# Maxima split on ACT and DVE, turned among the scores; the sums' input in five loads; a new order

## The chip, the cores and the metric

The kernel runs on one core of a Trainium2 chip. A core has a matrix engine (PE), three engines for element-wise work (DVE, ACT, POOL), a queue for transfers (SP) and 16 DMA engines. Times are microseconds of the device for one execution, and for a kernel the median of its runs.

## The reference

Attention over 8 batches of 8 heads with 576 positions of 64 columns, then a soft mixture of 8 experts with 4 slots each on the 4608 tokens of 512 columns:

```python
scores = scale * np.matmul(q, k.transpose(0, 1, 3, 2))
cum = np.cumsum(np.maximum(s, 0.0), axis=-1)
bias = -(cum[:, :, :, None] - cum[:, :, None, :])
scores = np.where(causal, -1000000000.0, scores + np.minimum(bias, 0.0))
scores = scores - np.max(scores, axis=-1, keepdims=True)
attn = np.exp(scores); attn = attn / (np.sum(attn, axis=-1, keepdims=True) + 1e-09)
x = np.matmul(attn, v)                       # heads side by side: 4608 x 512
logits = x @ phi                             # 4608 x 32
d = softmax over tokens of logits;  slot_input = d.T @ x
slot_out[e] = np.maximum(slot_input[e] @ w1[e], 0.0) @ w2[e]
out = (softmax over slots of logits) @ slot_out
```

The decay needs the running sums of s for every head before the first score can be formed, and the softmax needs each row's maximum before the scores that are exponentiated.

## The kernel before, in words

Two heads make a pair (32 pairs), and each pair's work is a set of steps. Head a of a pair lies in rows 64a to 64a + 63 of a tile, so a product over the 64 columns of a head uses half of the PE's rows, and two of them run side by side (tile shape 64*128 in the profile). q and k are cast to a rounded format on ACT (`cast`, L344), and what the rounding lost is kept by DVE (`low`, L349), one step each for q and k.

Each pair's scores are formed twice. First, in rounded numbers and with queries as rows, for the row maxima only (`mx`, L378, in four groups of which each fills two banks of PSUM); DVE takes the maxima (`red`, L389). The maxima, 5 chunks of 128 queries for two heads, are split into a rounded and a remaining part by two small operations on POOL (`f0`, L404 and L405), turned by the PE (`f1`; L425, one product on a tile of 128 rows and 64 columns; L421 for pair 0), copied by ACT (`f2`, L429) and moved by DMA into rows 32, 33, 96 and 97 of the tile `g`, whose rows 0, 1, 64 and 65 hold the running sums. Then the scores are formed again with keys as rows (`s`, L461, four products per block, the last with `g`), now less the maximum, and ACT exponentiates them (`ex`, L472). POOL clears what lies above the diagonal (`cut`, L479) and adds the blocks for the row sums (`z`, L507 to L513). The PE multiplies with v (`ax`, `a`: L560, L571, tile 128*64) and sums (`sm`, L599, 128*32), DVE scales the result (`nr`, L632), the PE turns it (`nat`) and forms logits (`lt`).

At the start s comes in by three loads (L202 to L204): heads 2 to 63 in rows 2 to 63, and heads 0 and 1 twice each into rows 0, 1 and 64, 65, which is where pair 0 wants them. DVE takes the maximum with zero (L227), the running sums (L228), their rounded part (L231) and writes `g` of pair 0 (L257); a POOL memset (L271) sets rows 32 and 33 of it to -1, after DVE's. The products of pair 0's maxima wait for both.

Six banks of PSUM go round in a ring for all products but the two longest-lived. The PE's order is given by a table of numbers (`PR`: first, phase, last); on the other engines a planner (`schedule`) runs through the steps with a duration each and takes the step that can start first, or the one with the smallest due time (also from `PR`). The outcome is written out as a fixed program per engine. Where the plan has the PE idle ahead of pair 0's weighted sums, filler products (L991) are put in.

## Time and profile before

| | us |
|---|---|
| median of 3 runs | 443.04 (441.56 to 446.37) |
| profiled execution | 437.39 |
| its span, first to last instruction | 435.4 |
| PE, DVE, POOL, ACT busy in the span | 413.4, 319.2, 281.7, 249.0 |
| first product that contains the sums | 12.5 |
| weights of the experts: first product | 373.5 |

A busy PE is a PE with products in flight; the ends of pipelined products are modelled, so the distance between two starts tells more of one product than its time. Idle time of an engine counts only where another one waits for it.

### The profile page before, as it was taken

Reading aid. Unit: us, or ns where it says so; the run is one execution under the profiler, and the core shown is the slowest. Engines: PE = TensorE matmul, PEld = TensorE weight load, DVE = VectorE, ACT = ScalarE, POOL = GpSimd, SP = SyncE. Lnnn points to the kernel's source line nnn. Section 1 sums busy time; section 2 is a strip of 40 time slices with the busy share of each in tenths; the row PEclk is TensorE's granted clock in tenths of the full one; section 3 lists DMA queues with packets and bytes.
Section 4 is the critical chain, followed back from the end, with each engine's and each line's share of the span. In section 5 each row is a group of like instructions: output and inputs, shape, how many; then the busy total and the mean of one; then the engine's idle time right before and its main releaser. Section 6 shows DMA issues by size and latency. Waiting matters only on the chain.

```text
span 435.4 us, 14712 instructions
## 1 busy us (share of the span) xinstructions
PE 413.4 (95%) x5708; PEld 302.1 (69%) x5708; DVE 319.2 (73%) x1039; ACT 249.0 (57%) x741; POOL 281.7 (65%) x389
## 2 busy tenths in 40 slices
PE   7899999999999999999999999999997999999990
PEld 7677777777687778777877687678775786345450
DVE  4899788878797889788978898789859555120570
ACT  2265766686667656765686577656773564111470
POOL 5769798968978788778877887679677930000000
PEclk9899999999999999999999999999999999999996
DMA  6317446762675257525853684253336879997898
GB/s 172 96 57 232 138 140 195 212 230 86 171 224 167 85 162 238 161 85 160 229 173 95 159 231 114 83 159 98 105 91 170 250 231 400 408 409 312 271 336 265
DMA packets 54174, 82.72 MB, mean 190 GB/s; under 512 B 5358, under 2 KB 41562, under 8 KB 54104
## 3 DMA queue, kind: packets, MB, share of 16 engines
q1 hardware_dynamic: 54104, 81.78, 60.0%
q8 instruction: 45, 0.74, 0.7%
q14 instruction: 25, 0.20, 0.2%
HBM read 71.39 MB, written 10.03 MB: 187 GB/s over the span
## 4 chain that ended last, share of the span: by engine, by line
PE 70%; DVE 10%; DMA 10%; issue 3%; POOL 2%; SPq 2%; ACT 1%; DVEq 0%; ACTq 0%
PE s L461 19%; PE y L571 15%; PE mx L378 10%; DMA arena<-rs 5%; PE m L1060 3%; PE sum L599 3%; PE po L1094 3%; PE m L1031 3%; DVE w L349 3%; DVE junk L389 3%; PE nat L640 3%; DMA rs<-sr 2%; PE sl L844 2%; DMA arena<-in_s_dram 2%; PE lt L713 1%
## 5 line engine op out<-in xcount | busy, mean ns | idle before, releaser
L472 ACT ACTIVATE arena<-s 128x288 f32<-128x288 f32 (+4 forms) x384 | 119.6, 393 | 74.4 <-PE s L461 73.2
L389 DVE CUSTOM_DVE_ANT_0 junk<-mx,mask 128x448 uint8<-128x448 f32 (+2 forms) x320 | 118.6, 424 | 17.7 <-PE mx L378 16.8
L461 PE MATMUL s<-w 64*128 64x288 f32 (+4 forms) x1152 | 110.6, 299 | 3.1 <-DVE mx L389 2.9
L571 PE MATMUL y<-arena 128*64 128x512 f32 (+4 forms) x640 | 97.2, 430 | 0.0
L461 PEld LDWEIGHTS s<-w 64*128 64x128 f32 (+1 forms) x1152 | 87.5, 176 | 12.2 <-DVE mx L389 5.8
L479 POOL TENSOR_SCALAR_AFFINE_SELECT arena<-arena 128x256 f32<-128x256 f32 (+1 forms) x160 | 67.0, 437 | 32.5 <-ACT arena L472 32.3
L349 DVE TENSOR_TENSOR w<-arena,w 128x576 fp32r<-128x576 f32 x64 | 83.9, 1330 | 3.5 <-ACT w L344 3.3
L507 POOL TENSOR_TENSOR arena<-arena 128x896 f32<-128x896 f32 x31 | 67.1, 2163 | 10.2 <-PE sum L599 8.5
L378 PE MATMUL mx<-w 64*128 64x288 f32 (+4 forms) x384 | 64.1, 317 | 2.0 <-ACT w L344 1.4
L461 PE MATMUL s<-g 64*128 64x288 f32 (+4 forms) x384 | 64.0, 291 | 0.2 <-DMA g<-hl 0.2
L571 PEld LDWEIGHTS y<-arena 128*64 128x64 f32 x640 | 39.4, 136 | 33.9 <-issue 26.0
L509 POOL TENSOR_TENSOR arena<-arena 128x640 f32<-128x640 f32 x31 | 55.3, 1784 | 2.0
L378 PE MATMUL mx<-g,ones 64*128 64x288 f32 (+4 forms) x384 | 55.2, 303 | 1.0 <-POOL g L271 1.0
L344 ACT CAST w<-arena 128x576 fp32r<-128x576 f32 x64 | 41.4, 676 | 16.9 <-DMA arena<-in_qk_dram 16.9
L378 PEld LDWEIGHTS mx<-w 64*128 64x128 f32 x384 | 39.8, 185 | 13.6 <-issue 4.3
L461 PEld LDWEIGHTS s<-g 64*128 64x128 f32 (+1 forms) x384 | 42.7, 177 | 1.2 <-DMA g<-hl 0.5
L632 DVE TENSOR_TENSOR arena<-arena 128x576 f32<-128x576 f32 x30 | 32.5, 1082 | 13.7 <-DMA arena<-rs 13.5
L378 PEld LDWEIGHTS mx<-g,ones 64*128 64x128 f32 x384 | 39.9, 187 | 1.7 <-POOL g L271 1.3
L511 POOL TENSOR_TENSOR arena<-arena 128x384 f32<-128x384 f32 x31 | 34.6, 1115 | 0.5
L389 DVE CUSTOM_DVE_ANT_0 junk<-mx,mask,mx 128x288 uint8<-128x288 f32 x64 | 30.0, 504 | 2.0 <-PE mx L378 1.8
L389 DVE DVE_READ_ACCUMULATOR2_ANT mx<- 128x1 f32 x384 | 31.0, 81 | 0.0
L404 POOL TENSOR_SCALAR mh<-mx 128x10 fp32r<-128x10 f32 x32 | 17.2, 539 | 16.0 <-DVE mx L389 15.7
(168 smaller groups left out, 539.2 us busy)
## 6 DMA issues: line engine op xcount, KB each, us to landing
arena<-in_qk_dram SPq DMA_DIRECT2D x32, 576.0 KB
pre<-in_w_dram SPq DMA_DIRECT2D x35, 512.0 KB
arena<-in_w_dram SPq DMA_DIRECT2D x18, 512.0 KB
arena<-rs SPq DMA_DIRECT2D x60, 144.0 KB
arena<-in_v_dram SPq DMA_DIRECT2D x32, 256.0 KB
out_dram<-arena SPq DMA_DIRECT2D x11, 512.0 KB
ww<-in_w_dram SPq DMA_DIRECT2D x7, 512.0 KB
wg<-in_w_dram SPq DMA_DIRECT2D x4, 512.0 KB
```

The source lines that it names most:

```text
L344: nc.scalar.copy(part(i), st["raw", p][:, i, :])
L349: nc.vector.tensor_tensor(part(2 + i), st["raw", p][:, i, :], part(i).bitcast(F32), op=ALU.subtract)
L378: nc.tensor.matmul(ps[a][:, d:d + hi - lo], l[r], t[r, KO + lo:KO + hi], start=t is w, stop=t is gt)
L389: nc.vector.tensor_tensor_reduce(out=junk[:, a, k:k + w], in0=ps[:, d:d + w], in1=mask[:, o:o + w], scale=1.0, scalar=m[:, a, 4:5] if i == ...
L461: nc.tensor.matmul(ps[a][0:n, d:d + hi - lo], t[r, ko + 128 * j:ko + 128 * j + n], t[r, qo + lo:qo + hi], start=x == 0, stop=x == 3)
L472: nc.scalar.activation(st["p", p][0:n, a, o + lo:o + hi], ps[0:n, d:d + hi - lo], AF.Exp, bias=0.0, scale=0.125)
L479: nc.gpsimd.affine_select(d, d, pattern=[[0, 2], [1, n]], compare_op=ALU.is_ge, fill=0.0, base=0, channel_multiplier=-1)
L507: eng.tensor_tensor(z[:, :, 128:576], pt[:, :, 128:576], pt[:, :, 576:1024], op=ALU.add)
L509: eng.tensor_tensor(z[:, :, 256:576], z[:, :, 256:576], pt[:, :, 1024:1344], op=ALU.add)
L511: eng.tensor_tensor(z[:, :, 384:576], z[:, :, 384:576], pt[:, :, 1344:1536], op=ALU.add)
L571: nc.tensor.matmul(y[r, lo - 64:512], vt[:, j, r], st["p", p][:, g, OFF[j] + lo - 128 * j:OFF[j] + 576 - 128 * j], start=(j == 0), stop=(j ...
L632: nc.vector.tensor_tensor(u, u, st.pop(("r", p)), op=ALU.mult)
```

## The change

Five things change. (1) s comes in by five loads: heads 0 and 1 twice each, then 30, 30 and 2 heads; heads 32 and 33 move to rows 66 and 67, rows 32 and 33 hold -1 throughout, and so DVE writes the whole of `g` of pair 0 and the POOL memset behind it is gone. The first maxima wait for DVE's set-up alone. The sums' copy to memory goes in three transfers. (2) The maxima are split by ACT (`fh`, a copy) and DVE (`f0`, a subtraction). (3) They are turned by two products on half rows, one for each half of 64 queries, into two banks; ACT copies them in two pieces. (4) The planner keeps one time for a port that DVE steps with two inputs in SBUF and POOL steps hold in turn: a step marked `port` starts no earlier than the last such one ended. Durations of steps are changed in a dozen places (by up to 0.8 us). (5) All numbers of the table `PR` are new, so the order is new on every engine.

```diff
-PR = dict(load=-2708.8403, load_v=1055.8902, cast=(823.0986, 1016.176), cum=-2520.1417,
...
+PR = dict(load=1107.499, load_v=998.6149, cast=(1514.9315, 1120.6562), cum=574.2308,
...
 PER = 1000
...
     mode = None
-    dma = 0
+    dma = port = 0
     index = {k: i for i, k in enumerate(ops)}
...
                 gap = 0 if e != "PE" else max(2, o["ldw"] - tail) if o["mode"] == mode else 100 + o["ldw"]
-                r = max(ready[k], f + gap)
+                r = max(ready[k], f + gap, port if o["port"] else 0)
                 n = o["bank"]
...
         free[e] = end
+        if o["port"]:
+            port = end
         if e == "PE":
...
-    begin = reg("p", NPB - 1)[0:66]
+    begin = reg("p", NPB - 1)[0:68]
     s_sb, ones_s, cum = begin[:, 0:S], begin[:, S:2 * S], begin[:, 1600:1600 + S]
-    nc.sync.dma_start(out=s_sb[2:64], in_=s[2:64])
-    nc.sync.dma_start(out=s_sb[0:2], in_=s[0:1].broadcast_to([2, S]))
-    nc.sync.dma_start(out=s_sb[64:66], in_=s[1:2].broadcast_to([2, S]))
+    for a in range(2):
+        nc.sync.dma_start(out=s_sb[64 * a:64 * a + 2], in_=s[a:a + 1].broadcast_to([2, S]))
+    heads = [(2, 2, 30), (34, 34, 30), (66, 32, 2)]
+    for r, h, n in heads:
+        nc.sync.dma_start(out=s_sb[r:r + n], in_=s[h:h + n])
+    nc.vector.memset(s_sb[32:34], 0.0)
     nc.vector.memset(ones_s, 1.0)
...
         mx.append(one.tile([128, 2, NCH], F32, name=f"mx{i}"))
-    mhs = [one.tile([128, 64], F32R, name=f"mh{i}") for i in range(2)]
-    ident1 = one.tile([128, 128], F32R, name="ident1")
-    nc.vector.tensor_copy(ident1, ident)
+    mhs = [one.tile([128, 128], F32R, name=f"mh{i}") for i in range(2)]
+    half1 = one.tile([128, 64], F32R, name="half1")
+    for a in (0, 64):
+        nc.vector.tensor_copy(half1[a:a + 64], ident[a:a + 64, a:a + 64])
     odd = one.tile([128, 1], F32, name="odd")
     nc.vector.scalar_tensor_tensor(odd, ident[:, 1:2], -1.0, ident[:, 65:66], op0=ALU.mult, op1=ALU.subtract)
     nc.vector.tensor_scalar(s_sb, s_sb, 0.0, 8.0, op0=ALU.max, op1=ALU.mult)
+    nc.vector.memset(s_sb[32:34, 0:1], -1.0)
     nc.vector.tensor_tensor_scan(out=cum, data0=ones_s, data1=s_sb, initial=0.0,
...
     ginit(0)
-    nc.vector.scalar_tensor_tensor(gs[0][0:66, KO:], cumhl[:, 0, :], odd[0:66], cum, op0=ALU.mult, op1=ALU.add)
+    nc.vector.scalar_tensor_tensor(gs[0][0:66, KO:], cumhl[0:66, 0, :], odd[0:66], cum[0:66], op0=ALU.mult, op1=ALU.add)
     ws = []
...
         nc.gpsimd.memset(reg("p", i).rearrange("p (a x) -> p a x", a=2)[64:128, :, 1536:1600], 0.0)
-    nc.gpsimd.memset(gs[0][32:34, KO:].bitcast(F32), -1.0)
     OFF = [0, 576, 1024, 1344, 1536]
     st = {}
     ops = {}
     live = {}
-    def op(key, eng, ns, prio, fn, after=(), bank=0, frees=None, dma=0, ldw=107, tail=107, mode=0, lat=0):
+    def op(key, eng, ns, prio, fn, after=(), bank=0, frees=None, dma=0, ldw=107, tail=107, mode=0, lat=0, port=0):
...
         ops[key] = dict(eng=eng, ns=ns, prio=round(t, 6), fn=fn, after=[a for a in after if a is not None], bank=bank,
-                        frees=frees or [], dma=dma, pt=prio, ldw=ldw, tail=tail, mode=mode, lat=lat)
+                        frees=frees or [], dma=dma, pt=prio, ldw=ldw, tail=tail, mode=mode, lat=lat,
+                        port=port or eng == "POOL" and key[0] not in ("set", "gi"))
...
             op(("cast", p, i), "ACT", 565, (tu, ("cast", i)), (cast, i), [("load", p)] + war)
-            op(("low", p, i), "DVE", 820, (t0, ("low", i)), (low, i), [("cast", p, i)])
+            op(("low", p, i), "DVE", 750, (t0, ("low", i)), (low, i), [("cast", p, i)], port=1)
...
             op(("cum", p), "SP", 720, (tu, "cum"), cum, war + [("lo",) if p < HP else ("cw",)] + ([("gi", p)] if 0 < p < NG else []), dma=60)
-        cums = [("cum", p) if p else ("set", "POOL")]
+        cums = [("cum", p) if p else ("set", "DVE")]
...
-        def f0():
+        def fh():
             use("mx", p, 3)
             mh = mhs[p % 2][:, 0:4 * NCH].rearrange("p (a l c) -> p a l c", a=2, l=2)
-            nc.gpsimd.tensor_scalar(mh[:, :, 0, :], m, 1.0, None, op0=ALU.mult)
-            nc.gpsimd.tensor_tensor(mh[:, :, 1, :], m, mh[:, :, 0, :].bitcast(F32), op=ALU.subtract)
+            nc.scalar.copy(mh[:, :, 0, :], m)
             st["mh", p] = mh
-        op(("f0", p), "POOL", 850, (tu, "f0"), f0, [("red", p, i, a) for i in range(4) for a in range(2)] + [dep("f1", old(2))])
+
+        def f0():
+            mh = st["mh", p]
+            nc.vector.tensor_tensor(mh[:, :, 1, :], m, mh[:, :, 0, :].bitcast(F32), op=ALU.subtract)
+        op(("fh", p), "ACT", 110, (tu, "fh"), fh, [("red", p, i, a) for i in range(4) for a in range(2)] + [dep("f1", old(2))])
+        op(("f0", p), "DVE", 160, (tu, "f0"), f0, [("fh", p)], port=1)
...
                 return
-            ps = st["mt", p] = bank("mt")
-            nc.tensor.matmul(ps[0:64, 0:128], mhs[p % 2], ident1, start=True, stop=True)
+            ps = st["mt", p] = bank("mta"), bank("mtb")
+            for a, r in enumerate(half):
+                nc.tensor.matmul(ps[a][:, 0:64], mhs[p % 2][r], half1[r], start=True, stop=True)
         def f2():
             hl = p2.tile([4 * NCH, 128], F32R, tag="hl", name=f"hl{p}", bufs=1)
-            nc.scalar.copy(hl, st.pop(("mt", p))[0:4 * NCH, 0:128])
+            for a, ps in enumerate(st.pop(("mt", p))):
+                nc.scalar.copy(hl[:, 64 * a:64 * a + 64], ps[0:4 * NCH, 0:64])
             st["hl", p] = hl
...
         if p:
-            op(("f1", p), "PE", 55, (tu, "f1"), f1, [("f0", p)], bank=1, ldw=53, tail=53, mode=2)
-            op(("f2", p), "ACT", 160, (tu, "f2"), f2, [("f1", p), dep("md", p - 1 or None)], frees=[(("f1", p), 0)])
+            op(("f1", p), "PE", 110, (tu, "f1"), f1, [("f0", p)], bank=2, mode=1)
+            op(("f2", p), "ACT", 220, (tu, "f2"), f2, [("f1", p), dep("md", p - 1 or None)], frees=[(("f1", p), x) for x in range(2)])
             op(("md", p), "SP", 1390, (tu, "md"), md, [("f2", p)], dma=60)
...
         for i in range(4):
-            op(("z", p, i), "POOL" if p < NP - 1 else "DVE", zt[i], (t0, ("z", i)), (zs, i), zd[i] + [("z", p, i - 1) if i else ("zc", p)])
+            op(("z", p, i), "POOL" if p < NP - 1 else "DVE", zt[i], (t0, ("z", i)), (zs, i), zd[i] + [("z", p, i - 1) if i else ("zc", p)], port=1)
...
-    for e, ns in (("DVE", 7000), ("POOL", 7300), ("SP", 1100), ("ACT", 2900), ("PE", 1100)):
+    for e, ns in (("DVE", 7450), ("POOL", 6500), ("SP", 1500), ("ACT", 2900), ("PE", 1100)):
         op(("set", e), e, ns, (-1000,), lambda: None)
     op(("lo",), "DVE", 750, (0.,), lambda: nc.vector.tensor_tensor(cumhl[:, 1, :].bitcast(F32R), cum, cumhl[:, 0, :], op=ALU.subtract),
-       [("set", "DVE")])
+       [("set", "DVE")], port=1)
     for i in range(1, NG):
...
     op(("cst",), "SP", 400, (61.0,), (fetch, cst_sb, cst), [("red", NP - 1, i, a) for i in range(4) for a in range(2)], dma=450)
-    op(("cw",), "SP", 400, (2.5,), lambda: nc.sync.dma_start(out=cumd, in_=cumhl[0:NH]), [("cum", 1)], dma=800)
+    op(("cw",), "SP", 1200, (2.5,), lambda: [nc.sync.dma_start(out=cumd[h:h + n], in_=cumhl[r:r + n]) for r, h, n in heads], [("cum", 1)], dma=800)
     op(("phi",), "SP", 900, (2.0,), load_phi, [("load", 2)], dma=300)
```

The first place is the start of the program. The order on SP (each row is an issue; `in_s` the sums' input, `in_qk` q and k of a pair, `in_v` v), before:

```order
L202 DMA arena<-in_s_dram 62x576
L203 DMA arena<-in_s_dram 2x576
L204 DMA arena<-in_s_dram 2x576
L335 DMA arena<-in_qk_dram 128x1152 x2
L540 DMA arena<-in_v_dram 128x4x128
L543 DMA arena<-in_v_dram 64x128
```

and now:

```order
L203 DMA arena<-in_s_dram 2x576 x2
L206 DMA arena<-in_s_dram 30x576 x2
L206 DMA arena<-in_s_dram 2x576
L340 DMA arena<-in_qk_dram 128x1152
L551 DMA arena<-in_v_dram 128x4x128
L554 DMA arena<-in_v_dram 64x128
L551 DMA arena<-in_v_dram 128x4x128
L554 DMA arena<-in_v_dram 64x128
L340 DMA arena<-in_qk_dram 128x1152
```

The load of q and k for pair 1 has moved behind those of v for pairs 0 and 1, and pair 0's has two more loads ahead of it.

DVE at the same place, from the sums' arrival to the first maximum (`g`: the operand with the sums; L349 and L354 `low`), before:

```order
L227 TENSOR_SCALAR arena<-arena 66x576
L228 SCALAR_TENSOR_TENSOR arena<-arena 66x576
L231 CAST arena<-arena 66x576
L257 SCALAR_TENSOR_TENSOR g_127<-arena,odd 66x576
L349 TENSOR_TENSOR w_136<-arena,w_136 128x576
L914 TENSOR_TENSOR arena<-arena 66x576
L389 ISA junk,mx_107<-mx_0_0_189,mask 128x288
```

and now:

```order
L231 TENSOR_SCALAR arena<-arena 68x576
L232 MEMSET arena 2x1
L233 SCALAR_TENSOR_TENSOR arena<-arena 68x576
L236 CAST arena<-arena 68x576
L262 SCALAR_TENSOR_TENSOR g_132<-arena,odd 66x576
L354 TENSOR_TENSOR w_141<-arena,w_141 128x576
L925 TENSOR_TENSOR arena<-arena 68x576
L394 ISA junk,mx_110<-mx_0_0_191,mask 128x288
```

A memset of two elements is added ahead of the running sums; nothing else moved here.

The second place is the PE around the turning of pair 12's maxima (`y`: weighted sums; `mx_13`: maxima of pair 13), before:

```order
L571 MATMUL y_2411<-arena 64x320 x2
L571 MATMUL y_2411<-arena 64x192 x2
L571 MATMUL y_2411<-arena 64x64 x2
L425 MATMUL mt<-ident_112,mh_110 64x128
L378 MATMUL mx_13_0_2444<-w_138 128x288
L378 MATMUL mx_13_1_2445<-w_138 128x288
```

and now:

```order
L582 MATMUL y_2446<-arena 64x320 x2
L582 MATMUL y_2446<-arena 64x192 x2
L582 MATMUL y_2446<-arena 64x64 x2
L435 MATMUL mta<-half_115,mh_113 128x64
L435 MATMUL mtb<-half_115,mh_113 128x64
L383 MATMUL mx_13_0_2478<-w_143 128x288
L383 MATMUL mx_13_1_2479<-w_143 128x288
```

Two products with half the columns stand for the one, at the same place between the weighted sums and the next pair's maxima.

The third place is DVE at the last low parts, those of pair 31 (`w2`), and the maxima of pair 30 (`mx1_30`, `mx2_30`, `mx3_30`: group and pair, then head), before:

```order
L389 ISA junk_121,mx0_107<-mx1_30_1_5955,mask_60,mx0_107 128x288
L389 ISA mx0_107 128x1
L349 TENSOR_TENSOR w2_138<-arena_76,w2_138 128x576 x2
L389 ISA junk_121,mx0_107<-mx3_30_0_6000,mask_60 128x320
L389 ISA mx0_107 128x1
L389 ISA junk_121,mx0_107<-mx3_30_0_6000,mask_60 128x192
L389 ISA mx0_107 128x1
L389 ISA junk_121,mx0_107<-mx3_30_1_6001,mask_60 128x320
L389 ISA mx0_107 128x1
```

and now:

```order
L394 ISA junk_126,mx0_110<-mx2_30_0_6075,mask_60 128x448
L394 ISA mx0_110 128x1
L394 ISA junk_126,mx0_110<-mx2_30_0_6075,mask_60 128x64
L394 ISA mx0_110 128x1
L394 ISA junk_126,mx0_110<-mx2_30_1_6076,mask_60 128x448
L394 ISA mx0_110 128x1
L394 ISA junk_126,mx0_110<-mx2_30_1_6076,mask_60 128x64
L394 ISA mx0_110 128x1
L354 TENSOR_TENSOR w2_143<-arena_76,w2_143 128x576
L414 TENSOR_TENSOR mh0_113<-mx0_110,mh0_113 128x2x5
L354 TENSOR_TENSOR w2_143<-arena_76,w2_143 128x576
```

All maxima of pair 30 have moved ahead of these low parts (group 3 stands further up), and the subtraction of pair 30 (L414) is between the two of them.

## Rows read from the trace of the kernel before

**Rows 1.** The page, part 4: shares of the chain of waits that ended last, by engine.

```profile
PE 70%; DVE 10%; DMA 10%; issue 3%; POOL 2%; SPq 2%; ACT 1%; DVEq 0%; ACTq 0%
```

**Rows 2.** Busy us of each engine by stretch, granted clock, DMA share, GB/s.

```profile
13.00:40.00 27.00, 25.87 (x292) 21.02 (x290) 25.23 (x99) 13.56 (x38) 20.39 (x31) 0.94 0.41 119
40.00:345.00 305.00, 300.88 (x4359) 227.95 (x4356) 253.68 (x834) 198.17 (x600) 245.84 (x325) 1.00 0.53 157
...
372.00:435.40 63.40, 51.64 (x583) 24.95 (x583) 20.00 (x52) 18.73 (x51) 0.46 (x1) 0.93 0.93 331
```

**Rows 3.** Timeline of the start: start us, us, engine, line, operation [idle before].

```profile
0.79 0.37 SPq L202 DMA_DIRECT2D arena<-in_s_dram  x1
...
1.42 8.30 PE L991 MATMUL busy<-ident 128*128 128x128 f32 x48 [1.42 <-POOL ident masks.py:199]
...
1.82 0.84 SPq L335 DMA_DIRECT2D arena<-in_qk_dram  x2
...
8.58 0.46 DVE L227 TENSOR_SCALAR arena<-arena 66x576 f32<-66x576 f32 x1 [4.62 <-DMA arena<-in_s_dram]
...
9.79 1.24 ACT L344 CAST w<-arena 128x576 fp32r<-128x576 f32 x2 [7.72 <-DMA arena<-in_qk_dram]
...
11.91 0.57 POOL L271 MEMSET g<- 2x576 f32 x1 [4.80 <-DVE g L257]
...
12.53 0.40 PE L378 MATMUL mx<-g,ones 64*128 64x288 f32 x2 [1.04 <-POOL g L271]
...
13.22 0.46 DVE L389 CUSTOM_DVE_ANT_0 junk<-mx,mask 128x288 uint8<-128x288 f32 x1
...
15.15 0.35 SPq L335 DMA_DIRECT2D arena<-in_qk_dram  x1
...
19.17 1.25 ACT L344 CAST w<-arena 128x576 fp32r<-128x576 f32 x2 [6.52 <-DMA arena<-in_qk_dram]
```

**Rows 4.** Timeline, end of pair 0's maxima and their split on POOL.

```profile
18.42 0.09 DVE L389 DVE_READ_ACCUMULATOR2_ANT mx<- 128x1 f32 x1
...
20.05 0.25 POOL L404 TENSOR_SCALAR mh<-mx 128x10 fp32r<-128x10 f32 x1
```

**Rows 5.** Timeline of PE: a change of tile, and the turning product.

```profile
102.52 0.40 PE L378 MATMUL mx<-w 64*128 64x288 f32 x2
102.75 0.30 PE L378 MATMUL mx<-g,ones 64*128 64x288 f32 x2
102.89 0.60 PE L461 MATMUL s<-w 64*128 64x320 f32 x6
...
343.10 0.27 PE L425 MATMUL mt<-ident,mh 128*64 128x128 f32 x1
343.30 0.71 PE L599 MATMUL sum<-arena,onesl 128*32 128x72 f32 x32
```

**Rows 6.** First low part (timeline), then groups by form: count, busy us, mean ns, idle before.

```profile
11.77 0.75 DVE L349 TENSOR_TENSOR w<-arena,w 128x576 fp32r<-128x576 f32 x1
...
L349 DVE TENSOR_TENSOR w<-arena,w 128x576 fp32r<-128x576 f32 x64 | 83.9, 1330 | 3.5 <-ACT w L344 3.3
...
L824 DVE SCALAR_TENSOR_TENSOR tot<-tot,al,mm 128x2 f32<-128x2 f32 x8 | 3.2, 404 | 4.3 <-ACT dt L818 4.3
...
L507 POOL TENSOR_TENSOR arena<-arena 128x896 f32<-128x896 f32 x31 | 67.1, 2163 | 10.2 <-PE sum L599 8.5 <-POOL arena L479 0.9 <-ACT arena L472 0.3
...
L404 POOL TENSOR_SCALAR mh<-mx 128x10 fp32r<-128x10 f32 x32 | 17.2, 539 | 16.0 <-DVE mx L389 15.7
...
L405 POOL TENSOR_TENSOR mh<-mx,mh 128x10 fp32r<-128x10 f32 x32 | 9.8, 306 | 2.7
...
L579 ACT COPY arena<-x 128x64 f32<-128x64 f32 x32 | 6.6, 210 | 15.9 <-PE x L560 15.7
```

**Rows 7.** Timeline around the longest wait of the scores for a bank.

```profile
325.78 4.98 DVE L349 TENSOR_TENSOR w<-arena,w 128x576 fp32r<-128x576 f32 x2
...
331.50 0.24 PE L461 MATMUL s<-w 64*64 64x64 f32 x1 [1.47 <-DVE mx L389]
```

56 lines of the change are left out of this document (27 added, 29 removed).

## The prediction

> **What bounds the kernel now.** I read the chain of waits first, then the busy time by stretch, then the first 23 us of the timeline, then single groups. The chain that ends last lies on the PE for 70% of the span, on DVE and DMA for 10% each [rows 1]; there is no one long wait in it. The stretches say the same from the other side: from 40 to 345 us the PE is busy 300.88 of 305 us, DVE 253.68, ACT 198.17, POOL 245.84 [rows 2]. So in the long middle only two things can pay: less work in the PE's own stream, and the 4.1 us in which it stands still. Ahead of the middle it is otherwise: the first product that contains the sums starts at 12.53 us and the first maximum at 13.22 us [rows 3], and until then the PE only runs filler products. From 13 to 40 us DVE is busy 25.23 of 27 us [rows 2]: the start is DVE's, so what lets DVE begin earlier moves everything behind it. After 372 us the expert weights and the output have the DMA engines at 0.93 of their time [rows 2]; that part is not edited and starts when the attention ends.
>
> **The start.** The sums arrive late: their loads are issued from 0.79 us, and DVE's first operation on them starts at 8.58 us after 4.62 us of idling [rows 3]. The two loads of q and k, 576 KB each, are issued from 1.82 us and ACT begins on it at 9.79 us. A later one of the same 576 KB with less around it, issued at 15.15 us, is used at 19.17 us: 4.0 us [rows 3]. So 139.5 KB of sums taking longer than 576 KB is a matter of shape (62 rows), and the five loads of the change cut 62 into 30, 30 and 2, after two of two rows. Five issues at up to 0.37 us each end by 2.7 us; with 4.0 us as the most that they should need, the sums are there by 6.7 us, 1.9 us earlier. From DVE's first step to the sums' operand being written it is 8.58 to 11.9 us, 3.3 us [rows 3], so by 10.0 us; the POOL memset of 0.57 us behind it, for which the PE waited until 12.53, goes, and a memset of two elements comes in. q and k, of which only the first pair is now ahead of v, should be cast by about 2.7 + 4.0 + 1.24 = 7.9 us. What is left is PE's own filler, unchanged in length, 1.42 + 8.30 = 9.7 us [rows 3]. The first full product then starts near 10.0 us: a gain of 2.5 us, of which DVE passes all on, being saturated behind it. Bounds: nothing, if the sums come no sooner (and 0.5 us lost, since q and k are issued behind two more loads of some 0.25 us); 2.8 us, down to the filler's end.
>
> The Trainium skill bears on this ("DMA: Bandwidth & Descriptors", section "Why a DMA increments its semaphore by 16 and not by 1"): a DMA runs on the largest number of engines, at most 16, that divides its slowest dimension. By that rule 62 rows go over 2 engines and 30 rows over 15, and the start's gain would be the whole 2.8 us; by the rows alone it could be nothing.
>
> One more thing goes at the start. Pair 0's maxima are complete at 18.5 us, but POOL, still clearing operands, splits them only at 20.05 us [rows 4]. With ACT and DVE doing it that is 1.5 us sooner; but DVE has other work queued in that time, so I count 0.5 us (0 to 1.5).
>
> **The turning product.** Before, it is one product on a tile of 128 rows by 64 columns; its neighbours run on half rows (scores, maxima) or on other tiles. From its start to its successor's it takes 343.30 - 343.10 = 0.20 us [rows 5]. After, it is a pair of half-row products of 64 columns, the tile of the scores. The nearest row is a half-row pair of 288 columns among its like, 102.75 to 102.89, 0.14 us; 64 of 288 columns of that are 0.03 us, but the weights to be loaded are no fewer. I take 0.1 us, nearer to the row: 31 x 0.1 = 3.1 us less. Against it stands the new order of the PE. Counted over the order up to the experts, the tile's shape changes 195 times before and 209 times after. The price of a change: the first pair of 288 columns takes 102.75 - 102.52 = 0.23 us behind a change and the second 0.14 us, so 0.1 us on entry [rows 5]; with as much for draining the old tile, 0.2 us. 14 x 0.2 = 2.8 us more. The PE's stream thus ends 0.3 us shorter; bounds -3.9 us (the changes cost only their entry, the pair 0.03 us) and +0.9 us (the pair costs 0.14 us).
>
> **The split.** POOL loses 17.2 + 9.8 = 27.0 us of small operations [rows 6]. ACT gains 32 copies and 31 evictions more than before; at 0.21 us, its shortest copy from the neighbourhood, that is 13 us on an engine with 305 - 198 = 107 us free in the middle: nothing, by that cover. SP gains two issues at the start (counted) and two for the sums' copy in memory; what is behind those on its queue, loads for pairs 2 and up, is not waited for before the PE is through with two pairs: nothing. The turned maxima now fill two of the six banks until ACT has copied them, not one, 31 times; the PE never waited for ACT's copies of them, so nothing, and its price if the banks run short is in the bounds of the idle time below. DVE gains 32 subtractions. The nearest row, a DVE step of two columns with two inputs, is 0.40 us [rows 6]: 13 us, covered by DVE's 51 us of idle time in the middle. Queued behind each subtraction are maxima, whose banks the PE waits for, and it waits itself for ACT's copy. If the cover is gone, up to 13 us lie on the path.
>
> **Order of DVE and POOL.** The low parts take DVE 1330 ns in the mean of 64 [rows 6], and 0.75 us in the first of all, beside which POOL only clears [rows 6]; the difference, 64 x 0.58 = 37 us, is DVE standing until a POOL operation ends. The one place where it reaches the PE at full size: at 325.78 DVE starts two low parts that take 4.98 us, the maxima of pair 30 stand behind them, and the PE's scores wait 1.47 us for a bank at 331.50 [rows 7]. In the new order all maxima of pair 30 stand ahead of the last low parts, and the plan holds a port's time free for each such operation, with POOL 27 us emptier. The PE's idle time in the middle is 4.1 us; I take 2.5 of it as gained (4.1 at most; and as a loss up to 4 us, as much again, for waits that the new order makes).
>
> **Sum.** -2.5 - 0.5 - 0.3 - 2.5 = -5.8 us. The profiled execution, 437.39 us, would become 431.6; it lies 5.65 us (1.3%) below the median of the three runs, 443.04, on which the forecast is put: **437 us**.
>
> **The rivals.**
> - *The start does not move* (the loads still land after 8 us, or q and k come late). For it: the change's q and k of pair 1 are issued behind v, later than before. Against: 576 KB need 4.0 us. Only the memset's 0.6 us stays: -0.6 - 0.3 - 2.5, 439.6 us. Chance 0.15.
> - *The idle time is only moved.* For it: the waits that remain are mostly short ones for banks, and any order has some. Then -2.5 - 0.5 - 0.3 = 439.7 us. Chance 0.25.
> - *Slower: the subtraction holds DVE up.* It stands in DVE's queue between maxima; if POOL is in one of its adds (2163 ns in the mean [rows 6]) it waits for the rest of it, and the maxima with it, and the PE runs out of banks. Each group takes two of six banks, so the PE is at most three groups ahead, 3 x 0.37 = 1.1 us of its time (102.52 to 102.89 [rows 5]). It decides when the subtraction with its wait is longer than that: half an add and its own 0.40 us are 1.5 us, so each costs the PE 0.4 us, 31 x 0.4 = 12.4 us, less 3.3 us from the first terms: 452 us. Against it: POOL's own small operations waited in the same way (539 ns in the mean for ten columns) without harm, and the plan now counts with the exclusion. Chance 0.1. The Trainium skill states the mechanism ("SBUF — State Buffer", section "Who interferes with whom"): a DVE operation with two inputs in SBUF and a POOL operation that reads SBUF block one another for a whole instruction. The two low parts of 4.98 us show it here; by that rule each of the 32 subtractions is exposed.
> - My forecast has 0.5.
>
> **Range and chances.** The terms' bounds give 443.04 - 2.8 - 1.5 - 3.9 - 4.1 = 430.7 us at the low end; on the high side the two rivals at 439.6 and some of the losses (+0.9 on the PE, +2 of the 4 in the middle) give 442.5. A measurement of this kernel can tell about 1% from no change, 4.4 us. The forecast's case lies beyond that with most of its weight (0.42 of 0.5), the first two rivals mostly within (0.12 of their 0.4 beyond it), the last slower: faster 0.54, same 0.35, slower 0.11.
>
> **What would show it.** The start: the first maximum on DVE near 10.7 us, not 13.2, and DVE's first step on the sums before 7 us. The turning: start to start of the pair near 0.1 us. The order: low parts near 0.9 us in the mean, and PE idle time in the middle under 2 us. The slower case would show as subtractions of over 1 us on DVE with maxima behind them and score products waiting for DVE. What would make it wrong: a first product that waits for q and k, or a middle that is longer between the same two pairs' products although its idle time is not.

## The result, and the profile after

| | before | after |
|---|---|---|
| median of the runs made with the prediction (4 each) | 442.30 us | 425.86 us, ratio 0.9665 (95% interval 0.9577 to 0.9752) |
| the changed kernel once more, beside the last experiments | 438.47 us | 426.64 us, ratio 0.9721 (0.9666 to 0.9775) |
| profiled execution, and its span | 437.39, 435.4 us | 424.91, 423.2 us |

The change makes the kernel faster, by 12 to 16 us and not by 6. The range of the prediction began at 431; the time lies below it.

The busy time by stretch of the changed kernel (us, then PE, weight loads, DVE, ACT and POOL busy, granted clock, DMA share, GB/s):

```profile
13.00:40.00 27.00, 26.46 (x319) 21.06 (x320) 24.07 (x106) 15.10 (x48) 16.33 (x21) 1.00 0.50 150
40.00:345.00 305.00, 301.87 (x4544) 234.65 (x4542) 239.97 (x856) 209.89 (x680) 226.20 (x274) 1.00 0.57 164
```

Beside [rows 2] the middle has 3.1 us of PE idle time in place of 4.1: the PE stands still almost as long as before. DVE is busy 14 us less although it has the subtractions as well, and POOL 20 us less. The column that moves with the time is another: the weight loads' busy time in the same 305 us is 234.65 in place of 227.95, 2.9% more. Taken as work that passed through the PE, that is worth 305 - 305/1.029 = 8.7 us. It is a rough figure: the turning itself loads weights for 3.85 us of this stretch before and, with two products in place of one, for 6.38 us after.

The timeline of the start of the changed kernel (start, us, operation, [idle before]):

```profile
1.54 1.07 SPq L206 DMA_DIRECT2D arena<-in_s_dram  x3
...
5.32 0.56 DVE L231 TENSOR_SCALAR arena<-arena 68x576 f32<-68x576 f32 x1
...
6.62 1.24 ACT L349 CAST w<-arena 128x576 fp32r<-128x576 f32 x2 [4.53 <-DMA arena<-in_qk_dram]
...
10.05 0.30 PE L383 MATMUL mx<-g,ones 64*128 64x288 f32 x2
...
10.38 0.46 DVE L394 CUSTOM_DVE_ANT_0 junk<-mx,mask 128x288 uint8<-128x288 f32 x1 [0.23 <-PE mx L383]
...
14.95 0.20 ACT L409 CAST mh<-mx 128x10 fp32r<-128x10 f32 x1 [1.77 <-DVE mx L394]
...
15.36 0.17 DVE L414 TENSOR_TENSOR mh<-mx,mh 128x10 fp32r<-128x10 f32 x1
```

Against [rows 3]: DVE's first step on the sums is 3.3 us earlier, the cast 3.2 us, the first full product 2.5 us, the first maximum 2.8 us; the split of pair 0 begins on ACT at 14.95 us, not on POOL at 20.05 [rows 4].

Two lines of the PE's timeline show how far the gain had grown: pair 0's first score product and the first product of the experts' input, in the changed kernel, and below them in the kernel before.

```profile
18.61 0.79 PE L472 MATMUL s<-w 64*128 64x448 f32 x6
...
359.22 1.08 PE L1031 MATMUL sit<-mask,acc 128*128 128x32 f32 x8 [0.73 <-ACT e_nat L801]
```

```profile
23.01 0.36 PE L461 MATMUL s<-w 64*64 64x64 f32 x6
...
372.01 1.08 PE L1020 MATMUL sit<-mask,acc 128*128 128x32 f32 x8 [0.73 <-ACT e_nat L790]
```

The first score product is 4.4 us earlier, the end of the attention 12.8 us, the end of the span 12.2 us: up to the first score product the change gains 4.4, in the middle 8.4, and the tail gives 0.6 back. In the middle the offset grows little by little; no single wait carries it. The one great stall of before [rows 7] is gone.

The groups by form (count | busy us, mean ns | idle before) that answer to [rows 6]:

```profile
L354 DVE TENSOR_TENSOR w<-arena,w 128x576 fp32r<-128x576 f32 x64 | 52.2, 833 | 0.4 <-ACT w L349 0.4
L414 DVE TENSOR_TENSOR mh<-mx,mh 128x10 fp32r<-128x10 f32 x32 | 14.9, 464 | 1.8 <-ACT mh L409 1.7
L409 ACT CAST mh<-mx 128x10 fp32r<-128x10 f32 x32 | 6.4, 199 | 23.2 <-DVE mx L394 23.2
```

The low parts fell from 1330 to 833 ns, 31.7 us of DVE's time in all. The new subtractions take 14.9 us. The turning pair and its successor on the PE's timeline answer to [rows 5]:

```profile
61.16 0.29 PE L435 MATMUL mta<-half,mh 64*128 64x64 f32 x1
...
61.17 0.29 PE L435 MATMUL mtb<-half,mh 64*128 64x64 f32 x1
...
61.39 0.71 PE L610 MATMUL sum<-arena,onesl 128*32 128x72 f32 x32
```

From the pair's start to its successor's it is 0.23 us here and 0.15 at the next one (69.84 to 69.99 us). Over the whole trace it is 0.13 us at most places where scores or maxima follow and up to 0.28 where another tile follows; the 31 pairs take 6.3 us (one of them 0.83), the 31 single products before took 6.1. The pairs are no shorter; they start sooner behind the product ahead of them, by some 1.7 us in all against the changed kernel with neither split nor turning (part 5, the last row).

### The profile page after: what moved, and what is told of

It is laid out like the page before. It is cut to its first block, busy times and chain, and to the rows that moved or that the text cites. A ratio compares the mean times of both kernels' runs of the same rounds, so it can differ in the third digit from the quotient of the medians.

```text
span 423.2 us, 14675 instructions
## 1 busy us (share of the span) xinstructions
PE 405.0 (96%) x5745; PEld 301.5 (71%) x5745; DVE 305.0 (72%) x1074; ACT 254.3 (60%) x804; POOL 255.0 (60%) x324
## 4 chain that ended last, share of the span: by engine, by line
PE 85%; DVE 4%; DMA 4%; ACT 2%; SPq 1%; issue 1%; DVEq 0%; POOL 0%; POOLq 0%
PE s L472 21%; PE y L582 19%; PE mx L383 13%; PE sum L610 4%; PE m L1071 4%; PE po L1105 3%; PE m L1042 3%; PE nat L651 3%; PE busy L1002 3%; DMA arena<-rs 2%; PE sl L855 2%; PE lt L724 2%; DVE junk L394 1%; DMA arena<-in_qk_dram 1%; PE x L571 1%
## 5 line engine op out<-in xcount | busy, mean ns | idle before, releaser
L394 DVE CUSTOM_DVE_ANT_0 junk<-mx,mask 128x448 uint8<-128x448 f32 (+3 forms) x320 | 119.2, 425 | 33.6 <-PE mx L383 33.2
L490 POOL TENSOR_SCALAR_AFFINE_SELECT arena<-arena 128x256 f32<-128x256 f32 (+1 forms) x160 | 69.9, 457 | 68.4 <-ACT arena L483 62.2
L472 PE MATMUL s<-w 64*128 64x288 f32 (+4 forms) x1152 | 105.8, 297 | 0.3 <-DVE mx L394 0.3
L472 PEld LDWEIGHTS s<-w 64*128 64x128 f32 (+1 forms) x1152 | 84.4, 177 | 4.2 <-DVE mx L394 1.0
L472 PE MATMUL s<-g 64*128 64x288 f32 (+4 forms) x384 | 58.7, 290 | 0.0
L354 DVE TENSOR_TENSOR w<-arena,w 128x576 fp32r<-128x576 f32 x64 | 52.2, 833 | 0.4 <-ACT w L349 0.4
L520 POOL TENSOR_TENSOR arena<-arena 128x640 f32<-128x640 f32 x31 | 50.7, 1634 | 2.4
L349 ACT CAST w<-arena 128x576 fp32r<-128x576 f32 x64 | 40.7, 672 | 12.0 <-DMA arena<-in_qk_dram 12.0
L472 PEld LDWEIGHTS s<-g 64*128 64x128 f32 (+1 forms) x384 | 37.3, 177 | 0.4
L643 DVE TENSOR_TENSOR arena<-arena 128x576 f32<-128x576 f32 x30 | 25.1, 835 | 7.8 <-DMA arena<-rs 7.8
L610 PE MATMUL sum<-arena,onesl 128*32 128x72 f32 x1024 | 22.4, 228 | 0.0
```

What stands on the lines that cost most here:

```text
L349: nc.scalar.copy(part(i), st["raw", p][:, i, :])
L354: nc.vector.tensor_tensor(part(2 + i), st["raw", p][:, i, :], part(i).bitcast(F32), op=ALU.subtract)
L394: nc.vector.tensor_tensor_reduce(out=junk[:, a, k:k + w], in0=ps[:, d:d + w], in1=mask[:, o:o + w], scale=1.0, scalar=m[:, a, 4:5] if i == ...
L472: nc.tensor.matmul(ps[a][0:n, d:d + hi - lo], t[r, ko + 128 * j:ko + 128 * j + n], t[r, qo + lo:qo + hi], start=x == 0, stop=x == 3)
L490: nc.gpsimd.affine_select(d, d, pattern=[[0, 2], [1, n]], compare_op=ALU.is_ge, fill=0.0, base=0, channel_multiplier=-1)
L520: eng.tensor_tensor(z[:, :, 256:576], z[:, :, 256:576], pt[:, :, 1024:1344], op=ALU.add)
```

## The experiments

Theory A: the middle was gained by the order. It keeps DVE's low parts off POOL's additions, DVE frees the banks sooner, and the PE's waits for them had been hidden inside the recorded times of its products. Theory B: the middle was gained by the operations, the split taken off POOL and the turning in half rows. Each time is a median, with its ratio to the kernel before on the same chip; that median lay between 438.5 and 439.9 us.

**1. Order and operations apart.** The first kernel has the changed kernel's order, with the old operations in their places; the second has the old order and all the new operations.

```diff
 order_only, against the changed kernel (and the old start and turning)
-            nc.scalar.copy(mh[:, :, 0, :], m)
-            nc.vector.tensor_tensor(mh[:, :, 1, :], m, mh[:, :, 0, :].bitcast(F32), op=ALU.subtract)
+            nc.gpsimd.tensor_scalar(mh[:, :, 0, :], m, 1.0, None, op0=ALU.mult)
+            nc.gpsimd.tensor_tensor(mh[:, :, 1, :], m, mh[:, :, 0, :].bitcast(F32), op=ALU.subtract)
 work_only, against the kernel before: the same lines the other way, with the new start and turning
```

> The changed kernel's order on every engine, with the work of the kernel before put back into its places: three loads of the sums' input and POOL's two -1 rows, both steps of the maxima's split on POOL, one whole turning product and one copy. Theory A (the middle was gained by the order: the new table and the planner's exclusion rule let the vector engine free the banks earlier, and the old trace hid the waits for them inside the products' recorded times): about -8 us against the kernel before, near 434, with the offset growing from pair 10 on. Theory B (the middle was gained by the operations: the split taken off POOL and the products in half rows): within 2 us of the kernel before, 440 to 444, since the order alone has nothing to give, or slower because it was made for other operations.

> The kernel before with its own table, planner and order, and the new operations alone: five loads with the -1 rows by the vector engine, the split by ACT and the vector engine at the place of POOL's, two half-row turning products and two copies. Theory A: the start's gain of about 3.5 us and at most 2 us more, near 438. Theory B: nearly the whole gain, 427 to 430. A third possibility, that the operations are dearer in an order not made for them (the subtraction holds the vector engine up, two banks in place of one): 442 or more although the first maximum comes as early as in the changed kernel.

The order alone: 430.01 us, 0.9794 (0.9760 to 0.9828), 9.2 us faster. The operations alone: 445.17 us, 1.0133 (1.0099 to 1.0168), 6 us slower. Theory A holds for the first and B falls; the second went the third way that its expectation named. Between pair 0's first score product and the experts' input the order alone is 7.9 us shorter than the kernel before (341.1 and 349.0 us). The low parts follow the order and not the operations (the order alone, then the operations alone):

```profile
L350 DVE TENSOR_TENSOR w<-arena,w 128x576 fp32r<-128x576 f32 x64 | 51.0, 818 | 1.0 <-ACT w L345 1.0
```

```profile
L353 DVE TENSOR_TENSOR w<-arena,w 128x576 fp32r<-128x576 f32 x64 | 88.3, 1396 | 3.2 <-ACT w L348 3.0
```

The middle of the order alone, to be held against [rows 2]: the PE's idle time is 1.5 us, 2.6 less than before.

```profile
40.00:345.00 305.00, 303.50 (x4467) 233.14 (x4463) 230.43 (x843) 202.65 (x619) 243.47 (x329) 1.00 0.56 164
```

**2. The start.** The five loads and DVE's -1 rows put into the kernel before, and taken out of the changed one.

```diff
 start_only, against the kernel before
-    nc.sync.dma_start(out=s_sb[2:64], in_=s[2:64])
+    heads = [(2, 2, 30), (34, 34, 30), (66, 32, 2)]
+    for r, h, n in heads:
+        nc.sync.dma_start(out=s_sb[r:r + n], in_=s[h:h + n])
...
-    nc.gpsimd.memset(gs[0][32:34, KO:].bitcast(F32), -1.0)
 old_start, against the changed kernel: the same lines the other way
```

> The kernel before with the start alone changed (five loads, the -1 rows by the vector engine), everything else and the order as before. If the start is passed on to the end as the prediction has it: the first maximum near 10.4 us in place of 13.2 and -2.5 to -3.5 us at the end, near 439.5. If the idle time is only moved, because the stretch behind the first pair is bound by something else: less than 1 us, 441.5 to 443.

> The changed kernel with the old start put back (three loads, POOL's two -1 rows), all else and the order as changed. If the start's gain is its own and adds to the rest: 3 to 4 us slower than the changed kernel, near 429.5. If the new order gives the rest only together with the early start: 6 us or more, 432 and up.

434.42 us, 0.9897 (0.9862 to 0.9932): the start is worth 4.8 us by itself, a little more than expected. Without it the changed kernel takes 430.11 us, 0.9770 (0.9724 to 0.9815), 2 to 5 us more than with it, by the two measurements of the changed kernel (the intervals overlap with the second). So start and order add up, within these intervals. The trace of the start alone does not show it: in its execution (438.07 us, the longest of nine) the first score product comes at 18.37 us, 4.6 us earlier than before, but the experts' input at 371.91, only 0.1 us earlier. From 331.07 to 337.89 us the granted clock is 0.50 there (1.2 GHz), and in the kernel before it was 1.00 in the whole middle; other executions took up to 6 us less, and whether their clock fell in the same place is not known.

**3. POOL's additions, the suspected cause, taken away.** From the sixth pair on the first three of a pair handle 32 columns per half, in both orders; these kernels leave out part of the row sums.

```diff
 before_narrow_z and after_narrow_z, each against its own kernel
-            if i == 0:
+            if NZ <= p < NP - 1 and i < 3:
+                c = 128 * i + 128
+                eng.tensor_tensor(z[:, :, c:c + 32], z[:, :, c:c + 32], pt[:, :, c:c + 32], op=ALU.add)
+            elif i == 0:
```

> The kernel before, but from the sixth pair on POOL's first three additions of a pair handle 32 columns per half in place of 448, 320 and 192 (the sums of the exponentials are left out in part). Order and all other work as before. Theory A (the vector engine loses its time waiting for POOL's additions in the low parts, the banks come free late, and TensorE's products hide the waits): the low parts fall from 1.33 to about 0.8 us and the time by 6 to 9 us, 430 to 433. Rival (the low parts' waits lie in the vector engine's idle time, and the order of TensorE's products is what counts): the low parts fall as well, the time by less than 3 us, 436 and up.

> The changed kernel with the same cut of POOL's additions (the sums of the exponentials are left out in part), as the control: here the low parts' excess is 5 us in all. Theory A: at most 2 us faster than the changed kernel, 423 to 426. If it falls by 5 us or more, POOL's additions bind the middle in some other way than through the low parts.

In the old order 428.17 us, 0.9754 (0.9708 to 0.9800): 10.8 us faster. In the new order 421.52 us, 0.9602 (0.9559 to 0.9646): against the changed kernel's 0.9665 and 0.9721 that is 3 to 5 us. So the old order paid 6 to 8 us more for these additions than the new one does, most of the 9.2 us that the order alone brings. The cut removes POOL work that other engines wait for as well, so the two prices are not the lock alone; the difference between the orders is. The low parts and the middle of the old order with the cut:

```profile
L349 DVE TENSOR_TENSOR w<-arena,w 128x576 fp32r<-128x576 f32 x64 | 50.0, 799 | 6.0 <-ACT w L344 5.8
```

```profile
40.00:345.00 305.00, 303.89 (x4523) 233.31 (x4521) 213.03 (x840) 204.89 (x626) 130.62 (x332) 1.00 0.55 164
```

The PE's idle time in the middle falls by 3.0 us, from 4.1 to 1.1, and the kernel by 10.8. Most of the waits had been counted as busy: over the span the same 5708 products are 413.4 us of busy time before and 406.7 with the cut. One kind of product shows it (scores of 288 columns, the three of a block's four that read `w`; from 40 to 345 us, the kernel before and then the cut):

```profile
L461 PE MATMUL s<-w 64*128 64x288 f32 x348 | 39.6, 312 | 1.2 <-DVE mx L389 1.0
```

```profile
L461 PE MATMUL s<-w 64*128 64x288 f32 x360 | 37.2, 308 | 0.0
```

39.6 us for 348 products is 0.114 us each, 37.2 for 360 is 0.103, while one by itself is recorded with 312 and 308 ns: the product did not change, but one that waits a moment for its bank, behind a neighbour whose recorded end lies past its successor's start, leaves no gap in the records. One such wait, in the kernel before and then at the same place with the cut:

```profile
146.81 0.79 PE L378 MATMUL mx<-w 64*128 64x320 f32 x2
147.05 0.08 DVE L389 DVE_READ_ACCUMULATOR2_ANT mx<- 128x1 f32 x1
147.19 0.56 PE L378 MATMUL mx<-g,ones 64*128 64x320 f32 x2
```

```profile
144.95 0.32 PE L378 MATMUL mx<-w 64*128 64x320 f32 x2
```

Before, one head's half of the pair starts at 146.81 us and the other's at 147.19, when DVE has freed its bank; the PE reads as busy throughout. I counted such cases from 22 us behind pair 0's first score product to 20 us ahead of the experts' input: products that DVE released just before their start, and how much further they stand behind the product ahead of them than is usual for the two kinds (the lower quartile over six of the traces). Of this lateness 6.5 us lie inside recorded products in the kernel before, beside 3.9 us of idle time; with the order alone it is 1.1 and 0.8 us, with the cut 1.0 and none, in the changed kernel 0.7 and 2.1. The fall of the sum by 8.5 us with the order alone covers the 7.9 us by which its middle is shorter.

**4. The rule, the table, and both.** The planner's rule and durations in the kernel before, with its table; the new table there, without the rule; and the changed kernel with the rule switched off.

```diff
 rule_only, against the kernel before (with the changed kernel's durations and port marks)
-                r = max(ready[k], f + gap)
+                r = max(ready[k], f + gap, port if o["port"] else 0)
 table_only, against the kernel before: PR is the changed kernel's
 no_rule, against the changed kernel
-                r = max(ready[k], f + gap, port if o["port"] else 0)
+                r = max(ready[k], f + gap)
```

> The kernel before with its own operations and its own table of numbers, but its planner knows the exclusion of the vector engine's subtractions and POOL's work and has the changed kernel's durations. Theory A1 (the rule by itself places the low parts between POOL's additions): the low parts' excess over 0.75 us falls from 37 us to under 10 and the time from 439 to 430 to 433. Theory A2 (the new table is what gives it, the rule only lets a search see it): the order of TensorE is the old one, since its order comes from the table, so less than 3 us, 436 to 441, whatever the low parts do.

> The kernel before with its own operations and its own planner without the rule, but with the changed kernel's table. Theory A1: the low parts fall on POOL's additions again (excess 25 us and more) and the time stays within 3 us of 439. Theory A2: TensorE's order alone brings 5 us or more, 434 and less.

> The changed kernel with its table, operations and durations, but the planner's rule switched off (a subtraction of the vector engine and POOL's work may be planned at the same time). If the rule is what keeps the low parts off POOL's additions: their excess over 0.75 us rises from 5 us to 20 and more, and the time by 6 us or more, 432 and up. If the table and the durations do it: 424 to 428, the excess under 10 us.

The rule with the old table: 485.07 us, 1.1026 (1.0965 to 1.1087). The table without the rule: 450.76 us, 1.0287 (1.0232 to 1.0342). The changed kernel without the rule: 448.84 us, 1.0229 (1.0184 to 1.0274). Both theories of the first two fell: neither part is worth anything by itself, both cost. The low parts stay at 1119 ns in the first and 1201 in the second. A table is a set of priorities for one planner; that it makes a bad order under another is the plain reading, not tested further. The third went as its first case has it: without the rule the low parts take 1213 ns, against 833 with it. The order changes with the rule on every engine, so the 22 us are not the lock's alone. Its low parts, and the lock itself on its timeline:

```profile
L354 DVE TENSOR_TENSOR w<-arena,w 128x576 fp32r<-128x576 f32 x64 | 77.5, 1213 | 0.7 <-ACT w L349 0.7
```

```profile
308.15 2.10 POOL L518 TENSOR_TENSOR arena<-arena 128x896 f32<-128x896 f32 x1
...
308.74 4.16 DVE L354 TENSOR_TENSOR w<-arena,w 128x576 fp32r<-128x576 f32 x2
310.32 1.97 POOL L520 TENSOR_TENSOR arena<-arena 128x640 f32<-128x640 f32 x1
```

Two low parts, 1.50 us of work, take 4.16 us: each ends about 0.6 us after the addition beside it (310.25, 312.29). The largest sum among the PE's waits in this kernel from 40 us on (waited for: us, times, longest) is for banks that DVE frees:

```profile
PE s L472 <- DVE mx L394: 5.8, 11, 0.9
```

In the trace of the changed kernel no wait of the scores for a bank is left in the middle, and its timeline has two low parts in a gap of POOL's work:

```profile
304.49 1.55 POOL L520 TENSOR_TENSOR arena<-arena 128x640 f32<-128x640 f32 x1
...
307.20 0.45 POOL L524 TENSOR_TENSOR arena<-arena 64x128 f32<-64x128 f32 x1
310.43 1.36 DVE L354 TENSOR_TENSOR w<-arena,w 128x576 fp32r<-128x576 f32 x2
311.74 0.41 POOL L490 TENSOR_SCALAR_AFFINE_SELECT arena<-arena 128x256 f32<-128x256 f32 x1 [4.09 <-ACT arena L483]
```

**5. Split and turning one by one,** in the old order and in the new one. The edits are those of part 1 for the split; for the turning:

```diff
 turn_one, against the changed kernel (turn_only: the other way, in the kernel before)
-            ps = st["mt", p] = bank("mta"), bank("mtb")
-            for a, r in enumerate(half):
-                nc.tensor.matmul(ps[a][:, 0:64], mhs[p % 2][r], half1[r], start=True, stop=True)
+            ps = st["mt", p] = bank("mt")
+            nc.tensor.matmul(ps[0:64, 0:128], mhs[p % 2], ident1, start=True, stop=True)
```

> The kernel before in its own order, with the split of the maxima alone changed (ACT's copy and the vector engine's subtraction at the place of POOL's two steps). Theory S (the loss of the kernel with all new operations in the old order, 445 against 434 with the start alone, is the vector engine's: its subtraction waits in the queue for ACT's copy, and the maxima behind it wait too): 444 to 450. Theory T (the loss is the turning product's: a second bank and two copies in an order that counted one): 437 to 440.

> The kernel before in its own order, with the turning alone changed (two half-row products in two banks, two copies). Theory S: 436 to 440, since the product in the scores' own tile spares the change of tile but costs a bank. Theory T: 444 and more.

> The changed kernel and its order, with the split back on POOL (its two steps at the place of the vector engine's subtraction, nothing at the place of ACT's copy). If the split off POOL is worth something by itself: 2 us or more slower than the changed kernel, 428 and up. If it only fits the order (the two kernels with the old start, 430.0 and 430.1, differ in nothing): 424 to 427.

> The changed kernel and its order, with one whole turning product in one bank and one copy, as before. By the prediction's account the two half-row products save 3.1 us of change of tile: 428 to 429. By the start-to-start times of the two traces (the turning costs 7.4 and 7.5 us in all, its neighbours some 2 us less): 426 to 428. If a bank fewer helps: under 425.

> The changed kernel with its early start and its order, but with the split back on POOL and one whole turning product. If order and start are the whole gain: 424 to 427. If the two half-row products are worth the 2.5 us that their own removal showed (427.6): 427 to 429. If split and turning only pay together: 430 and more.

| | in the old order | the changed kernel without it |
|---|---|---|
| split | 449.84 us, 1.0224 (1.0182 to 1.0267) | 425.25 us, 0.9666 (0.9626 to 0.9707) |
| turning | 444.48 us, 1.0102 (1.0066 to 1.0138) | 427.56 us, 0.9731 (0.9686 to 0.9776) |
| both | | 426.23 us, 0.9722 (0.9690 to 0.9754) |

In the old order the split costs 10 us and the turning 4.5. In the new order neither can be told from nothing: all three kernels lie in the intervals of the changed one, which are some 4 us wide to either side in the first measurement and 2 in the second. As far as that tells, order and start are the whole gain.

**6. Why the split is dear in the old order.** One kernel lets DVE's subtraction stand later in the queue, behind other work; the other joins the split with the cut of part 3.

```diff
 split_late, against the kernel before with the split alone
-            nc.vector.tensor_tensor(mh[:, :, 1, :], m, mh[:, :, 0, :].bitcast(F32), op=ALU.subtract)
+            later.append((now[0] + 850, lambda: nc.vector.tensor_tensor(mh[:, :, 1, :], m, mh[:, :, 0, :].bitcast(F32), op=ALU.subtract)))
```

> The kernel before in its own order, with the split by ACT and the vector engine as in the run that did this alone (450), but the vector engine's subtraction stands 0.85 us later in the planned order, where POOL's second step would have ended, so that other work of the vector engine stands between ACT's copy and it. If the loss of 10 us was the wait in the queue for ACT's copy: 438 to 444. If it was the vector engine's added time (13 us of subtractions in an order in which it is late already): 447 and more.

> The kernel before in its own order with both edits: POOL's first three additions of a pair cut to 32 columns per half from the sixth pair on (the sums of the exponentials are left out in part), and the split of the maxima by ACT and the vector engine. The cut alone gave 428.2, the split alone 449.8. If the split is dear only because low parts that wait for POOL hold the vector engine up in front of its subtraction: within 3 us of the cut alone, 427 to 431. If the old order has no room for the subtraction in any case: the two add, 436 and more.

Later is worse: 461.19 us, 1.0536 (1.0494 to 1.0578). That lies in the second theory's open range, but not by its reason: the subtractions take 13.0 us of DVE, and 12.4 in the split alone, which is 11 us faster. With the cut the split costs nothing: 428.90 us, 0.9783 (0.9741 to 0.9825), against 428.17 for the cut alone. The waits of the PE say why (waited for: us, times, longest), for the split alone and then for the late one:

```profile
PE mt L425 <- DVE mh L405: 6.0, 6, 1.0
PE s L461 <- DVE mx L389: 3.7, 4, 1.5
```

```profile
PE mt L426 <- DVE mh L406: 11.3, 7, 2.5
PE s L462 <- DVE mx L390: 4.7, 6, 1.5
```

It is not the subtraction that holds the others up; it is held up. It stands in DVE's queue behind low parts that wait for POOL, and the turning product, at the head of the PE's queue, waits for it. POOL's own split did not have to pass DVE's queue. That DVE's lateness comes from POOL's additions is shown by the cut; how much of the 10 us each wait carries is open. A part of the loss can be the clock: with the late subtraction the granted clock is 0.94 in the mean of 170 to 360 us, where it was 1.00 in the kernel before, so up to 190 x 0.06 = 11 us of the 23 may be lost that way behind the PE's waits.

**7. What is left to be had.** The last of POOL's four additions of a pair goes to DVE.

```diff
 z3_dve, against the changed kernel
-            eng = nc.gpsimd if p < NP - 1 else nc.vector
+            eng = nc.gpsimd if p < NP - 1 and i < 3 else nc.vector
```

> The changed kernel and its order, with the last of POOL's four additions of a pair (64 by 128, 0.54 us on POOL, 16 us in all) by the vector engine, at the same place. If what POOL's additions still cost in the new order (3 us by the cut) can be had so: 422 to 425. If the vector engine's own time or a wait for POOL's addition before it costs as much: 425 to 430.

> The changed kernel once more, unchanged, on the chip of these runs: 0.966 of the kernel before, 424 to 426, if its first measurement (0.958 to 0.975) holds.

427.72 us, 0.9755 (0.9719 to 0.9791): no gain, perhaps a small loss. The changed kernel itself came out at 0.9721 this time. No version tried that computes the whole result beats it by more than the runs can tell.

## Why the prediction was wrong

- **The start** (-2.5 and -0.5 forecast): right in its steps and a little small. DVE's first step on the sums at 5.3 us, the first full product at 10.05 (10.0 forecast) and the first maximum at 10.38 (10.7) came as worked out, and the runs give 2 to 5 us. The first score product gained 1.6 us more than the first maximum (4.4 - 2.8), 0.5 of which was counted. Half of the 1.6 is the order: before, a low part of 0.75 us stood among pair 0's maxima (13.98 us), now it stands behind them. The other half is the split: from the last maximum to the turning it is 2.14 us before and 1.34 now. The granted clock differs as well, 0.94 from 13 to 40 us [rows 2] and 1.00 now: behind the PE's wait for the first full product it was at 0.50 (1.2 GHz) from 13.88 to 17.30 us. But DVE, on which the start waits, was busy 3.37 of these 3.42 us and the PE ran filler products from 15.32 us on, so a loss by the clock there is not shown. On the loads the Trainium skill's rule ("DMA: Bandwidth & Descriptors", section "Why a DMA increments its semaphore by 16 and not by 1") agrees with the trace: 62 rows were waited for until 8.58 us, loads of 30 rows had landed by 5.32. No run here shows on how many engines each went.
- **The turning product** (-3.1 for the products, +2.8 for changes of tile): the products were mis-sized, for 31 pairs take 6.3 us to their successors and not 3.1, against 6.1 for the single products. The runs cannot tell the turning's worth in the new order from nothing, so the sum of -0.3 stands by chance; the price of a change of tile (0.2 us) was not measured by itself.
- **The split at nothing:** right in the new order, and only there. The cover that I named, DVE's 51 us of idle time, was the wrong one: what matters is whether DVE is late when the maxima are complete.
- **The order: the step that failed.** The lock was read rightly (64 x 0.58 = 37 us of DVE's time, a mean near 0.9 us afterwards: 0.83 measured). But I let it pass on to the time only through the PE's idle time in the middle, of which I took 2.5 us as gained and 4.1 at most. With the order alone the idle time did fall by 2.6 us, but the kernel became 9.2 us faster; in the changed kernel it fell by 1.0 and the middle became 8.4 us shorter. The PE's recorded busy time is no measure of the work that it does: short waits between pipelined products lie inside it, 6.5 us of them for DVE in the kernel before (part 3). With the bound at 4.1 the low end of the range could not reach the result. The Trainium skill says of the distance to the roofline ("Perfetto Trace Analysis", section "Identifying the Most-Contended Engine") that matmul busy time is a poor measure because matmuls are pipelined, and that the share of peak FLOPs and the weight loads' busy share are to be used; of waits inside the busy time it says nothing. The traces agree in the direction: the weight loads were busy 227.95 of 305 us in [rows 2] and 234.65 after, worth 8.7 us where the timeline gives 8.4. The nearness is partly luck, for the turning's second load is in it; the order alone (233.14) gives 6.8 us by this measure and 7.9 by the timeline, the cut (233.31) 7.0 and 9.7. I had quoted the first column and not the second.
- **The rivals.** "The idle time is only moved" was wrong for the same reason. "The subtraction holds DVE up" (452 us) did not come in the changed kernel, but the split put into the old order makes it: 449.84 us. Its price was near (12.4 us forecast, 10 measured) and its last link wrong: the PE waits for the subtraction itself at the turning product, 6.0 us at six places, more than for banks (3.7); so the nearness is luck.
- **What would show it:** of the signs that I had named, the first maximum, DVE's first step and the low parts came; the turning near 0.1 us and an idle time under 2 us (3.1 measured) did not. As a sign of being wrong I had named a middle that becomes longer between the same two products although its idle time does not. The middle and the idle time did part, but to the good side.

## What to carry to other kernels

When a pipelined engine reads 99% busy, its idle time is no upper bound of what a late producer costs it: compare the time between the same two products in both kernels; busy time per identical product and weight loads in a fixed stretch point the same way, but only roughly. When two engines lock each other out, plan for it: the same operations in an order that keeps them apart were worth 9 us of 439, of which 6 to 8 go with the collisions, and the split and the turning changed beside it nothing that the runs can tell. Moving a small step to an engine with much idle time is free only if that engine is on time at that moment; and a table of priorities belongs to the planner that it was found with.

## What the runs showed of the hardware that I had not expected

A low part that starts during one of POOL's additions ends some 0.6 us after it (0.61 to 0.62 in the trace before), not 0.75: a small part of it overlaps, or POOL's recorded ends, which are rough, lie that much late. It is not only the additions: beside POOL's clearing above the diagonal a low part of 0.95 us occurs as well (62.77 us before). With 37 us lost in the old order (34 of 64 low parts over 0.9 us), 5.5 us are lost in the new one (10 of 64). POOL pays as well: the addition of 640 columns takes 1.97 us when it is issued during a low part (310.32; 1.94 to 1.96 in 12 of 13 such cases before) and 1.55 in the changed kernel's timeline without one (304.49). In the new order the choice of the engine for 64 by 128 additions or ten-column splits moves the end far less than the place of these collisions.
